# A linear-attention and SwiGLU kernel rewritten in hand order: four tokens per partition, attention pieces in slots beside FFN steps, DMA transposes, two-bank PSUM tiles

## The chip, the cores and the metric

The kernel runs on one core of one Trainium2 chip. The metric is device time in microseconds (us) of one execution; lower is better. Every number below comes from a timed run, from the profile of one execution, or is worked out from such numbers, and the text says how. The profile's span (first to last instruction) is up to 2 us shorter than the time. A run is called slow when it took over 1.5% longer than the fastest run of the same kernel. Verdicts and ratios use the fast runs alone; the medians in the tables are of all runs (the change, e5 and e12 have one slow run of four, e13 has two).

Engines are named as the profile names them: PE is TensorE (matmuls), PEld its weight loads, DVE is VectorE, ACT is ScalarE, POOL is GpSimd, SPq is the queue of SyncE, from which most DMAs are issued. PSUM is the memory that matmuls write into; a tile of 128 x 512 fp32, the size of one accumulator here, is called one bank. To evict a tile is to move its contents from PSUM to the on-chip memory SBUF, which DVE and ACT do here.

## The reference, cut to what matters

Linear attention over 8 batches, 8 heads, 576 tokens, head width 64, and then an RMS norm and a SwiGLU feed-forward network (FFN) over all 4608 tokens, 512 wide inside the model and 1536 wide in the FFN.

```python
def phi(x, c, s):
    r = np.maximum(x, 0.0)
    return np.concatenate([r * c, r * s], axis=-1)      # 64 -> 128 features
q_p, k_p = phi(q, cos_w, sin_w), phi(k, cos_w, sin_w)
kv  = np.einsum('bhsf,bhsd->bhfd', k_p, v)              # "kvz": with sum(k_p) as 65th column
num = np.einsum('bhsf,bhfd->bhsd', q_p, kv)             # "nd": numerator and denominator
x   = num / den, heads side by side                     # 4608 x 512
xn  = x / rms * rms_g
out = (silu(xn @ w_gate) * (xn @ w_val)) @ w_out
```

## The kernel before

The tile framework orders the instructions and sets the waits between engines. The FFN works on blocks of 512 tokens. While block b-1 is in its gate/value steps, batch b's attention and block b-2's output matmuls are interleaved. 576 tokens are 4.5 rows of 128, so batches and blocks don't align.

```python
psmm  = ctx.enter_context(tc.tile_pool(name="psmm", bufs=1, space=PSUM))
psgv  = ctx.enter_context(tc.tile_pool(name="psgv", bufs=2, space=PSUM))   # gps, vps: two tiles each
psacc = ctx.enter_context(tc.tile_pool(name="psacc", bufs=2, space=PSUM))  # acc: two tiles

def attn_kvz(b):                         # [cut] 5 chunks per head; the tail chunk has 64 rows
    for h in range(H):
        for ci, (ti, lane0, clen, s0, col, ridx) in enumerate(chunks):
            nc.tensor.matmul(kvz[:, h, 0 : FA + 1], lhsT=kp[:clen, ci, h, :],
                             rhs=vv[:clen, ci, h, :], start=(ci == 0), stop=(ci == len(chunks) - 1))

def ffn_gval_step(blk, nn, filler_blk=None):            # one of 12 steps of a block
    gps = psgv.tile([P, 512], FP32, name="gps", tag="g")
    vps = psgv.tile([P, 512], FP32, name="vps", tag="v")
    # [cut] 4 matmuls into gps, 4 into vps
    if filler_blk is not None:
        ffn_out_step(filler_blk, 4)                     # 4 output matmuls of an earlier block
    nc.scalar.activation(out=sig[:, :], in_=gps[:, :], func=AF.Sigmoid)
    nc.scalar.copy(out=valc[:, :], in_=vps[:, :])
    nc.vector.tensor_tensor(out=t1[:, :], in0=gps[:, :], in1=sig[:, :], op=ALU.mult)
    nc.gpsimd.tensor_tensor(out=hT[:, nn, :], in0=t1[:, :], in1=valc[:, :], op=ALU.mult)

for b in range(1, B):                                   # [cut]
    attn_prep(b, next_load=b + 1)        # casts, phi; q transposed on TensorE, evicted by DVE
    for nn in range(0, 4):  ffn_gval_step(b - 1, nn, b - 2)
    attn_kvz(b)
    for nn in range(4, 8):  ffn_gval_step(b - 1, nn, b - 2)
    attn_numden(b)
    for nn in range(8, 12): ffn_gval_step(b - 1, nn, b - 2)
    batch_finish()                       # norm; x transposed by DMA
    ffn_out_flush(b - 2)
```

Of the kernel before, what the change touches and what calls it, by code (L numbers as in the profile page):

```python
# [5 lines left out]

# [8 lines left out]
ALU = mybir.AluOpType  # L15


@with_exitstack
def kernel(
# [13 lines left out]
    T = B * S  # L33
# [3 lines left out]
    NTT = T // P  # L37
    TB = 512
    NBLK = T // TB
    NDT = DM // P  # L40
    NNT = DFF // P
    FA = D
    F = 2 * D
    assert B == 8 and H == 8 and S == 576 and D == 64
    inv_dm = 1.0 / DM

    consts = ctx.enter_context(tc.tile_pool(name="consts", bufs=1))
    wts = ctx.enter_context(tc.tile_pool(name="wts", bufs=1))
    raw_pool = ctx.enter_context(tc.tile_pool(name="raw", bufs=1))
    qp_pool = ctx.enter_context(tc.tile_pool(name="qp", bufs=2))  # L50
    kp_pool = ctx.enter_context(tc.tile_pool(name="kp", bufs=1))
    qpt_pool = ctx.enter_context(tc.tile_pool(name="qpt", bufs=1))
    kvz_pool = ctx.enter_context(tc.tile_pool(name="kvzs", bufs=2))
    xt_pool = ctx.enter_context(tc.tile_pool(name="xt", bufs=5))
    small = ctx.enter_context(tc.tile_pool(name="small", bufs=6))
    xn_pool = ctx.enter_context(tc.tile_pool(name="xn", bufs=4))
    xnt_pool = ctx.enter_context(tc.tile_pool(name="xnt", bufs=4))
    scr_pool = ctx.enter_context(tc.tile_pool(name="scrp", bufs=2))
    psmm = ctx.enter_context(tc.tile_pool(name="psmm", bufs=1, space=bass.MemoryType.PSUM))
    psgv = ctx.enter_context(tc.tile_pool(name="psgv", bufs=2, space=bass.MemoryType.PSUM))  # L60
    psacc = ctx.enter_context(tc.tile_pool(name="psacc", bufs=2, space=bass.MemoryType.PSUM))
    late = {}

    even_starts = [0, 128, 256, 384, 512]
    odd_starts = [0, 64, 192, 320, 448]
    s0_list = even_starts + odd_starts
    ncol = len(s0_list)
    iota_i = consts.tile([P, 1], mybir.dt.int32, name="iota_i")
    nc.gpsimd.iota(iota_i[:, :], pattern=[[0, 1]], base=0, channel_multiplier=1)
    iota_f = consts.tile([P, 1], FP32, name="iota_f")  # L70
    nc.vector.tensor_copy(out=iota_f[:, :], in_=iota_i[:, :])
    cos_tab = consts.tile([P, ncol], FP32, name="cos_tab")
    sin_tab = consts.tile([P, ncol], FP32, name="sin_tab")
    th_tab = consts.tile([P, ncol], FP32, name="th_tab")
    cth_tab = consts.tile([P, ncol], FP32, name="cth_tab")
    ang = math.pi / 2.0 / float(S)
    for j, s0 in enumerate(s0_list):
        nc.vector.tensor_scalar(
            out=th_tab[:, j : j + 1], in0=iota_f[:, :], scalar1=float(s0), scalar2=ang,
            op0=ALU.add, op1=ALU.mult,  # L80
        )
    nc.vector.tensor_single_scalar(
        out=th_tab[:, :], in_=th_tab[:, :], scalar=math.pi / 2.0, op=ALU.min
    )
    nc.vector.tensor_single_scalar(
        out=cth_tab[:, :], in_=th_tab[:, :], scalar=math.pi / 2.0, op=ALU.add
    )
    nc.scalar.activation(out=sin_tab[:, :], in_=th_tab[:, :], func=AF.Sin)
    nc.scalar.activation(out=cos_tab[:, :], in_=cth_tab[:, :], func=AF.Sin)
    ident = consts.tile([P, P], BF16, name="ident")  # L90
    masks.make_identity(nc, ident[:, :])

    raw_tiles = {}
    last_load = {}

    def issue_loads(b):
        rq4 = raw_pool.tile([P, 4, H, D], FP32, name="rq4", tag="rq4")
        rk4 = raw_pool.tile([P, 4, H, D], FP32, name="rk4", tag="rk4")
        rv4 = raw_pool.tile([P, 4, H, D], FP32, name="rv4", tag="rv4")
        rq1 = raw_pool.tile([P, H, D], FP32, name="rq1", tag="rq1")  # L100
        rk1 = raw_pool.tile([P, H, D], FP32, name="rk1", tag="rk1")
        rv1 = raw_pool.tile([P, H, D], FP32, name="rv1", tag="rv1")
        if b % 2 == 0:
            s4 = slice(0, 512)
            s1 = slice(512, 576)
        else:
            s1 = slice(0, 64)
            s4 = slice(64, 576)
        for (rr4, rr1, src) in ((rv4, rv1, v), (rk4, rk1, k), (rq4, rq1, q)):
            for c in range(4):  # L110
                s0 = s4.start + c * P
                nc.sync.dma_start(  # L112
                    out=rr4[:, c, :, :],
                    in_=src[b, :, s0 : s0 + P, :].rearrange("h s d -> s h d"),
                )
            ins = nc.sync.dma_start(
                out=rr1[0:64, :, :],
                in_=src[b, :, s1, :].rearrange("h s d -> s h d"),
            )
            last_load[b] = ins  # L120
        raw_tiles[b] = (rq4, rk4, rv4, rq1, rk1, rv1)

    wg = wts.tile([P, NDT, DFF], BF16, name="wg")
    wv = wts.tile([P, NDT, DFF], BF16, name="wv")
    wo = wts.tile([P, NNT, DM], BF16, name="wo")
    rmsg = consts.tile([P, NDT], FP32, name="rmsg")

    def weight_dmas(stage_pool):
        with nc.allow_non_contiguous_dma(reason="small gather of rms_g"):
            nc.sync.dma_start(  # L130
                out=rmsg[:, :], in_=moe_rms_g.rearrange("(t p) -> p t", p=P)
            )
        sgs, svs, sos = [], [], []
        for dt in range(NDT):
            sg = stage_pool.tile([P, DFF], FP32, name=f"sg{dt}", tag=f"sg{dt}")
            nc.sync.dma_start(out=sg[:, :], in_=moe_w_gate[dt * P : (dt + 1) * P, :])
            sgs.append(sg)
        for dt in range(NDT):
            sv = stage_pool.tile([P, DFF], FP32, name=f"sv{dt}", tag=f"sv{dt}")
            nc.sync.dma_start(out=sv[:, :], in_=moe_w_val[dt * P : (dt + 1) * P, :])  # L140
            svs.append(sv)
        for nt3 in range(NNT // 3):
            so = stage_pool.tile([P, 3, DM], FP32, name=f"so{nt3}", tag=f"so{nt3}")
            nc.sync.dma_start(
                out=so[:, :, :],
                in_=moe_w_out[nt3 * 3 * P : (nt3 + 1) * 3 * P, :].rearrange(
                    "(t p) m -> p t m", p=P
                ),
            )
            sos.append(so)  # L150
        return sgs, svs, sos

    def weight_convs(sgs, svs, sos):
        for dt in range(NDT):
            nc.vector.tensor_scalar(
                out=wg[:, dt, :], in0=sgs[dt][:, :], scalar1=rmsg[:, dt : dt + 1],
                scalar2=None, op0=ALU.mult,
            )
        for dt in range(NDT):
            nc.vector.tensor_scalar(  # L160
                out=wv[:, dt, :], in0=svs[dt][:, :], scalar1=rmsg[:, dt : dt + 1],
                scalar2=None, op0=ALU.mult,
            )
        for nt3 in range(NNT // 3):
            nc.scalar.copy(out=wo[:, nt3 * 3 : (nt3 + 1) * 3, :], in_=sos[nt3][:, :, :])

    def chunks_of_batch(b):
        i0 = (9 * b) // 2
        if b % 2 == 0:
            lst = [  # L170
                (i0 + 0, 0, 128, 0, 0, 0),
                (i0 + 1, 0, 128, 128, 1, 1),
                (i0 + 2, 0, 128, 256, 2, 2),
                (i0 + 3, 0, 128, 384, 3, 3),
                (i0 + 4, 0, 64, 512, 4, -1),
            ]
        else:
            lst = [
                (i0 + 0, 64, 64, 0, 5, -1),
                (i0 + 1, 0, 128, 64, 6, 0),  # L180
                (i0 + 2, 0, 128, 192, 7, 1),
                (i0 + 3, 0, 128, 320, 8, 2),
                (i0 + 4, 0, 128, 448, 9, 3),
            ]
        return lst

    xtok = {}
    xt_done = {}
    pending = []
    ssq_cur = {}  # L190
    xnT_blocks = {}
    hT_tiles = {}
    kp_tiles = {}
    vv_tiles = {}
    qpT_tiles = {}
    ssq_tiles = {}
    ksv_tiles = {}

    def ensure_xnT_block(blk):
        if blk not in xnT_blocks:  # L200
            t = xnt_pool.tile([P, NDT, TB], BF16, name=f"xnT_{blk}", tag="xnT")
            xnT_blocks[blk] = t
        return xnT_blocks[blk]

    def tile_complete(i, ssq_b):
        ensure_xnT_block(i // 4)
        col = len(pending)
        pending.append(i)
        xt = xtok[i]
        scr = scr_pool.tile([P, DM], FP32, name="scr", tag="scr")  # L210
# [5 lines left out]
    def batch_finish():  # L216
        tiles = list(pending)
        if not tiles:
            return
# [134 lines left out]
    def ffn_out_step(blk, nsteps):  # L354
# [3 lines left out]
        for _ in range(nsteps):  # L358
            if j >= 4:
                break  # L360
# [123 lines left out]
```

## Time and profile before

| | before |
|---|---|
| time, median of 3 | 423.27 us (422.99 to 423.47) |
| profile's span | 421.9 us |
| first FFN matmul | 65.4 us |
| one batch in steady state | 39.8 us |

The page's first part is the busy time of each engine (us, share of the span, number of instructions):

```profile
PE 345.4 (82%) x2215; PEld 174.3 (41%) x2256; DVE 259.3 (61%) x541; ACT 206.9 (49%) x419; POOL 127.3 (30%) x115
```

82% is an average of two regimes. The windows view gives busy time by stretch (columns: window, its length, then each engine's busy us and instructions, granted TensorE clock, DMA share, GB/s):

```profile
0.00:65.00 65.00, 12.41 (x128) 9.51 (x128) 37.47 (x99) 12.60 (x25) 0.76 (x7) 1.00 1.09 263
...
225.00:265.00 40.00, 38.84 (x269) 19.72 (x273) 30.52 (x63) 22.82 (x49) 15.24 (x13) 1.00 0.57 123
```

For 65 us PE has almost nothing to do, because data and weights are being loaded and prepared. Later it is busy most of the time.

The timeline of PE shows a late stretch in which the FFN runs alone (columns: start us, length us, engine, line, operation, output<-inputs, count, and in brackets the idle time before it and what ended it):

```profile
355.81 1.03 PE L394 MATMUL gps<-xnT_3368,wg 128*128 128x512 bf16 x4
356.68 1.03 PE L402 MATMUL vps<-xnT_3368,wv 128*128 128x512 bf16 x4
357.54 1.03 PE L364 MATMUL acc<-wo,hT 128*128 128x512 bf16 x4
358.40 1.03 PE L394 MATMUL gps<-xnT_3368,wg 128*128 128x512 bf16 x4
```

Read the starts, not the lengths: the length includes the tail of the pipelined matmul. From 355.81 to 356.68 to 357.54 to 358.40 each group of four takes 0.86 us, 216 ns per matmul, and nothing waits. A block of FFN is 144 such matmuls, 31.1 us.

One more line of the timeline, the 40 kvz matmuls of a batch:

```profile
199.18 2.96 PE L303 MATMUL kvz<-vv,kp 128*128 128x65 bf16 x40
```

### The profile page before, as it was taken

What the parts mean: (1) busy time and instruction counts of PE and PEld (TensorE: products, weight loads), DVE (VectorE), ACT (ScalarE), POOL (GpSimd) and SP (SyncE); (2) the same over time, 40 slices, a digit from 0 to 9 for tenths busy, and PEclk for the clock granted to TensorE, in tenths of its full rate; (3) what the DMA queues carried; (4) which work ended last, traced back from release to release, by engine and by line L of the source; (5) the groups of instructions that cost most, each with busy time, mean ns of one, the idle gap of its engine ahead of it and who ended that gap; (6) DMA issues with size and microseconds to landing.
All of it is one profiled execution on the core that took longest, in us unless ns stands there. A gap on an engine that the chain in (4) does not pass through costs nothing.

```text
span 421.9 us, 6418 instructions
## 1 busy us (share of the span) xinstructions
PE 345.4 (82%) x2215; PEld 174.3 (41%) x2256; DVE 259.3 (61%) x541; ACT 206.9 (49%) x419; POOL 127.3 (30%) x115
## 2 busy tenths in 40 slices
PE   0262008969897999979989999899999999999996
PEld 0241005534453445444444544454455444444442
DVE  3857547697469868775888596959681463222210
ACT  1004403546365644754465458544834686555541
POOL 0000001443145333424242434234243434444430
PEclk9999999989999999999999999999999999999999
DMA  9999999970676765736573675450120013010012
GB/s 178 225 416 394 214 176 187 198 155 2 123 170 124 157 152 128 149 86 138 125 164 76 127 163 113 110 115 26 39 63 26 26 50 88 27 50 26 25 50 99
DMA packets 140591, 52.32 MB, mean 124 GB/s; under 512 B 133392, under 2 KB 133392, under 8 KB 140560
## 3 DMA queue, kind: packets, MB, share of 16 engines
q1 hardware_dynamic: 140560, 51.92, 54.7%
q8 instruction: 17, 0.28, 0.3%
q14 instruction: 14, 0.11, 0.1%
HBM read 37.75 MB, written 9.44 MB: 112 GB/s over the span
## 4 chain that ended last, share of the span: by engine, by line
PE 59%; DVE 15%; DMA 11%; ACT 6%; issue 4%; SPq 4%; DVEq 0%; ACTq 0%
PE gps L394 17%; PE acc L364 16%; PE vps L402 15%; PE kvz L303 6%; PE tps L288 4%; SPq L112 3%; DMA rv_271<-in_v_dram 3%; PE nd L323 2%; DVE kp L269 2%; DVE kp L265 2%; DVE qp L278 2%; DVE qpT L291 2%; ACT sig L412 2%; DVE xt L342 1%; DVE xn L233 1%
## 5 line engine op out<-in xcount | busy, mean ns | idle before, releaser
L364 PE MATMUL acc<-wo,hT 128*128 128x512 bf16 x426 | 108.1, 379 | 0.4
L412 ACT ACTIVATE sig<-gps 128x512 bf16<-128x512 f32 x108 | 64.8, 600 | 74.5 <-PE gps L394 67.6
L414 ACT CAST valc<-vps 128x512 bf16<-128x512 f32 x108 | 63.2, 585 | 31.6 <-PE vps L402 30.1
L288 PE MATMUL tps<-ident,qp 128*128 128x128 bf16 (+1 forms) x320 | 26.0, 231 | 45.7 <-DVE qp L282 40.6
L394 PEld LDWEIGHTS <-wg 128*128 128x128 bf16 x432 | 40.4, 99 | 54.6 <-issue 8.9
L402 PEld LDWEIGHTS <-wv 128*128 128x128 bf16 x432 | 41.9, 99 | 47.2 <-issue 1.1
L364 PEld LDWEIGHTS <-hT 128*128 128x128 bf16 x432 | 41.2, 98 | 46.1
L288 PEld LDWEIGHTS <-qp 128*128 128x128 bf16 (+1 forms) x320 | 21.9, 106 | 57.9 <-DVE qp L282 42.6
L211 ACT ACTIVATE scr<-xt 128x512 f32<-128x512 f32 x36 | 22.7, 629 | 18.5 <-DVE xt L342 18.5
L323 PE MATMUL nd<-kvzs,qpT 128*128 128x65 bf16 (+1 forms) x320 | 18.4, 202 | 14.6 <-DVE xt L342 13.5
L374 ACT COPY osb<-acc 128x512 f32<-128x512 f32 x36 | 21.2, 588 | 18.2 <-PE acc L364 18.0
L291 DVE COPY qpT<-tps 128x1024 bf16<-128x1024 bf16 (+1 forms) x40 | 25.3, 633 | 6.7 <-PE tps L288 6.3
L342 DVE TENSOR_TENSOR xt<-nd,rec 128x512 f32<-128x512 f32 (+1 forms) x40 | 27.5, 688 | 1.0
L312 ACT CAST kvzs<-kvz 128x65 bf16<-128x65 f32 x64 | 8.3, 252 | 39.4 <-PE kvz L303 39.4
L323 PEld LDWEIGHTS <-qpT 128*128 128x128 bf16 (+1 forms) x320 | 14.8, 105 | 28.0 <-DVE xt L342 22.7
L303 PE MATMUL kvz<-vv,kp 128*128 128x65 bf16 (+1 forms) x320 | 24.8, 203 | 0.5 <-DVE qpT L291 0.5
L417 POOL TENSOR_TENSOR hT<-t_578,valc 128x512 bf16<-128x512 bf16 x1 | 1.2, 1151 | 70.4 <-DMA rv_547<-in_v_dram 70.4
L303 PEld LDWEIGHTS <-kp 128*128 128x128 bf16 (+1 forms) x320 | 18.1, 99 | 9.5 <-issue 2.6
L412 ACT ACT_TABLE_LOAD x8 | 10.3, 1283 | 22.2 <-PE gps L394 22.1
L233 DVE TENSOR_SCALAR xn<-xt,rs 128x512 bf16<-128x512 f32 x36 | 17.7, 547 | 1.3 <-DMA xnT_3368<-xn 0.6
L337 DVE RECIPROCAL rec<-nd 128x8 f32<-128x8 f32 (+1 forms) x40 | 8.1, 201 | 11.5 <-PE nd L323 11.4
L394 PE MATMUL gps<-xnT_353,wg 128*128 128x512 bf16 x45 | 13.3, 410 | 2.1 <-DMA xnT_353<-xn 1.4
(344 smaller groups left out, 568.6 us busy)
## 6 DMA issues: line engine op xcount, KB each, us to landing
out_dram<-osb SPq DMA_DIRECT2D x36, 256.0 KB, 2.1
rv_133<-in_v_dram SPq DMA_DIRECT2D x4, 256.0 KB, 4.7
rk_132<-in_k_dram SPq DMA_DIRECT2D x4, 256.0 KB, 5.5
rq_131<-in_q_dram SPq DMA_DIRECT2D x4, 256.0 KB, 5.3
rv_271<-in_v_dram SPq DMA_DIRECT2D x4, 256.0 KB, 9.6
rk_270<-in_k_dram SPq DMA_DIRECT2D x4, 256.0 KB, 5.9
rq_269<-in_q_dram SPq DMA_DIRECT2D x4, 256.0 KB, 5.9
rv_544<-in_v_dram SPq DMA_DIRECT2D x4, 256.0 KB, 4.2
```

What stands on the lines that cost most here:

```text
L211: nc.scalar.activation(out=scr[:, :], in_=xt[:, :], func=AF.Square, accum_out=ssq_b[:, col : col + 1])
L233: nc.vector.tensor_scalar(out=xn[:, :], in0=xt[:, :], scalar1=rs[:, jj : jj + 1], scalar2=None, op0=ALU.mult,)
L288: nc.tensor.transpose(tps[:, h, 0:clen], qp[:clen, h, :], ident[:clen, :clen])
L291: nc.vector.tensor_copy(out=qpT[:, :, s0 : s0 + clen], in_=tps[:, :, 0:clen])
L303: nc.tensor.matmul(kvz[:, h, 0 : FA + 1], lhsT=kp[:clen, ci, h, :], rhs=vv[:clen, ci, h, :], start=(ci == 0), stop=(ci == len(chunks) - 1),)
L323: nc.tensor.matmul(nd[lane0 : lane0 + clen, h, 0 : FA + 1], lhsT=qpT[:, h, s0 : s0 + clen], rhs=kvzs[:, h, :], start=True, stop=True,)
L342: nc.vector.tensor_tensor(out=xt3[lane0 : lane0 + clen, :, :], in0=nd[lane0 : lane0 + clen, :, 0:D], in1=rec[lane0 : lane0 + clen, 0:H].un ...
L364: nc.tensor.matmul(acc[:, :], lhsT=hT[:, nn, j * P : (j + 1) * P], rhs=wo[:, nn, :], start=(nn == 0), stop=(nn == NNT - 1),)
L394: nc.tensor.matmul(gps[:, :], lhsT=wg[:, dt, nn * P : (nn + 1) * P], rhs=xnT[:, dt, :], start=(dt == 0), stop=(dt == NDT - 1),)
L402: nc.tensor.matmul(vps[:, :], lhsT=wv[:, dt, nn * P : (nn + 1) * P], rhs=xnT[:, dt, :], start=(dt == 0), stop=(dt == NDT - 1),)
L412: nc.scalar.activation(out=sig[:, :], in_=gps[:, :], func=AF.Sigmoid)
L414: nc.scalar.copy(out=valc[:, :], in_=vps[:, :])
```

## The change

The intent is to rewrite the kernel with the order of instructions set by hand. Each partition holds four consecutive tokens, so loads move runs of 1 KB instead of 256 B. A block is the first 512 tokens of one batch, and the eight remainders of 64 tokens make a ninth, shared block. Attention pieces sit in named slots of the 16 steps of a block (12 gate/value steps, 4 output steps). Sigmoid, copy and two products become one Silu and one product; POOL keeps only the small rsqrt of the norm in the loop. The q transposes of batches 2 to 7 go to the DMA. The weights are cast by the DMA. The tail rows of kvz are padded with zeros to 128. All of PSUM is four tiles of two banks each, used half by half.

The diff, cut to its core:

```diff
+    ctx.enter_context(tc.manual_schedule())
-    psmm = ctx.enter_context(tc.tile_pool(name="psmm", bufs=1, space=bass.MemoryType.PSUM))
-    psgv = ctx.enter_context(tc.tile_pool(name="psgv", bufs=2, space=bass.MemoryType.PSUM))
-    psacc = ctx.enter_context(tc.tile_pool(name="psacc", bufs=2, space=bass.MemoryType.PSUM))
+    ps = ctx.enter_context(tc.tile_pool(name="ps", bufs=1, space=bass.MemoryType.PSUM))
+    psA = ps.tile([P, 2, 512], FP32, name="psA")      # kvz, nd
+    psG = ps.tile([P, 2, 512], FP32, name="psG")      # gate
+    psV = ps.tile([P, 2, 512], FP32, name="psV")      # value
+    psC = ps.tile([P, 2, 512], FP32, name="psC")      # output
@@ [cut: loads] @@
+            in_=src[b, h0:h1, 0:512, :].rearrange("h (p j) d -> p h (j d)", j=4),
@@ [cut: kvz; kpt and vvt are the tail chunk, padded with zeros] @@
+                lhsT = kp_main[b][:, c, h, :] if c < 4 else kpt[b % 2][:, h, :]
+                rhs = vvm[b % 2][:, c, h, :] if c < 4 else vvt[b % 2][:, h, :]
@@ [cut: FFN steps] @@
-        nc.scalar.activation(out=sig[:, :], in_=gps[:, :], func=AF.Sigmoid)
-        nc.scalar.copy(out=valc[:, :], in_=vps[:, :])
-        nc.vector.tensor_tensor(out=t1[:, :], in0=gps[:, :], in1=sig[:, :], op=ALU.mult)
-        nc.gpsimd.tensor_tensor(out=hT[:, nn, :], in0=t1[:, :], in1=valc[:, :], op=ALU.mult)
+        nc.scalar.activation(out=sg[:, :], in_=psG[:, bank, :], func=AF.Silu)
+        nc.vector.tensor_tensor(
+            out=hTs[blk][:, n, :], in0=psV[:, bank, :], in1=sg[:, :], op=ALU.mult)
@@ [cut: slots; k_phi and loads are placed in the same way] @@
+            at(b, qn, "post", q_phi, V, nb, c, 0)
+            at(b, qn, "post", q_phi, A, nb, c, 1)
+            at(b, qn, "post", q_tr_dma, nb, c)
+        at(vb, vn, "post", v_cast, A, nb, LOW)
+        at(vb, vn + 1 if first else vn, "post", v_cast, A, nb, HIGH)
+        at(vb, vn, "post", v_cast_tail, A, nb)
+    def gval_step(blk, n):
+        bank = n % 2
+        run(blk, n, "pe")
+        gval_mm(blk, n, bank)
+        run(blk, n, "pre")
+        sg = gval_act(blk, n, bank)
+        gval_h(blk, n, bank, sg)
+        run(blk, n, "post")
+    def out_step(blk, j):
+        n = 12 + j
+        run(blk, n, "pe")
+        bank = psC[:, j % 2, :]
+        for i in range(NNT):
+            out_mm(blk, j, i, bank)
+        run(blk, n, "pre")
+        out_store(nc.scalar, blk, j, bank)
+        run(blk, n, "post")
+    for blk in range(1, 9):
+        for n in range(NNT):
+            gval_step(blk, n)
+        for j in range(4):
+            out_step(blk, j)
```

## The prediction

> **What bounds it now.** TensorE. The page has PE busy 82% of 421.9 us; the windows show two regimes. Until 65.4 us there is no FFN matmul: PE works about 17 of 70 us. After that PE is busy about 95%, and successive last x transposes (145.9, 184.8, 224.6, 266.0, 303.5, 344.7 us in the timeline) give 39.8 us per batch. In the timeline four 128x512 matmuls take 0.863 us, 216 ns each; the Trainium skill (TensorE: Matmul & The Clock Gate, "Wait — 56ns, not 53.3ns?") states 215.7 ns, and this trace agrees. A block of FFN is 144 of them, 31.1 us; 40 kvz matmuls take 2.9 us; 40 nd 2.2; 40 q transposes 3.0: sum 39.2. So stalls are only about 0.6 us per batch. Nine FFN blocks alone are 280 us.
>
> **What the change does.**
> 1. q transposes leave PE for DMA in batches 2-7: -3.0 us of PE each, 18 us in all. A 128x512 DMA transpose takes 1.22 us of SP's queue; a 128x1024 should take near 2.4. I estimate 17 us of transposes per block plus 5 for loads and stores, of 36: it fits.
> 2. sig, valc, t1, hT become one Silu (ACT, 0.60) and one product (DVE, 0.69). POOL leaves the loop, so the phis that take 1.37 us beside POOL return to 0.48: the Trainium skill (SBUF — State Buffer, Terms, shared port pair) states such blocking; the trace is consistent with it. Table loads (16 x 1.28) go; half of phi moves to ACT. I estimate ACT 190 and DVE 185 us busy: neither binds, so nearly all of this is off the critical path.
> 3. The xnT wait between batches (1-2 us) goes: x is transposed during the output steps. The tail block collects the remainders.
> 4. Opening: 1 KB runs instead of 256 B, weights cast by the DMA, FFN started chunk by chunk. DMA moved 410 GB/s for weights but 180-210 for q, k, v. I estimate batch 0 landed near 13 us, FFN from about 25, then paced by PE and the loads (wo by 50-60 us). Block 0's output with batch 1's attention: 16 us of PE plus 8 of waits (transpose directly behind nd, square, norm). Block 0 done near 77 us; before, at 107, its output projection was still to be done.
>
> **Sum.** 77 (70-85) + 6 blocks x (31.1+2.9+2.2, plus 0.8 of stalls) = 222, + 2 bare blocks 62.2 + last copy and store 3 = 364. Against before: about 40 from the opening, 18 from transposes, the rest waits. Time 364 us, range 350 to 382. Faster by over 2%: 0.96; within 2%: 0.03; slower: 0.01.
>
> **What would show it.** Page: PE busy above 90%, total near 335 us; POOL below 5% after the opening. Timeline: first FFN matmul near 25 us, block 0's last output near 77, period 36-38 us. Chain of waits: almost all PE, DMA only in the first 60 us. Granted clock near 1.
>
> **What would make it wrong.** (a) 128x1024 DMA transposes cost more, or queue behind the 1 MB loads, so nd waits and the period exceeds 38. (b) Casting weight DMAs are slow, or batch 1's loads behind them stop the in-order DVE and ACT in block 0, and it ends past 85. (c) psA is the only buffer for kvz and nd: an nd waits for the eviction before it (0.69 + 0.4). (d) Silu slower, or table reloads. (e) PE idling long enough to lower its clock.

## The result, and the profile after

| | before | after |
|---|---|---|
| time, median | 423.32 us (4 runs) | 412.27 us (409.08 to 415.47, 4 runs; one slow) |
| ratio of fast runs | 1 | 0.972 (95% interval 0.966 to 0.978) |
| profile's span | 421.9 us | 408.5 us |
| mean granted clock in the profile | 0.990 | 0.956 |

Ratios here and below are the mean time of one kernel's fast runs over that of the kernel before in the same rounds, so they are not quite the ratios of the medians quoted. The change is faster, by 2.8% (12 us). The prediction was 364 us, 14% less than before, with 382 as the upper end of its range. Its direction was right; 48 us are missing.

The same line of the page after:

```profile
PE 341.2 (84%) x2085; PEld 162.3 (40%) x2122; DVE 180.1 (44%) x366; ACT 188.5 (46%) x345; POOL 38.3 (9%) x74
```

The predicted engine loads came true (ACT 190, DVE 185, PE about 335), and yet PE is at 84% and not above 90. So the missing time is not work. It is waiting. The windows view for the three stages (up to the end of block 0, blocks 1 to 6 with attention beside them, blocks 7 and 8 alone):

```profile
0.00:91.91 91.91, 62.24 (x485) 35.00 (x492) 43.24 (x97) 37.32 (x71) 22.74 (x46) 0.85 0.81 171
91.91:333.47 241.56, 212.85 (x1322) 99.50 (x1346) 120.29 (x245) 131.54 (x242) 15.59 (x28) 0.99 0.67 148
333.47:408.50 75.03, 66.07 (x282) 27.83 (x286) 16.60 (x24) 19.61 (x33) 0.00 (x0) 0.99 0.11 32
```

Set against the terms of the prediction's sum (starts of the blocks read from the timeline of PE):

| stage | predicted | after |
|---|---|---|
| to the end of block 0 | 77 | 91.9 |
| blocks 1 to 6 | 222 (37.0 each) | 241.4 (40.2 each) |
| blocks 7 and 8 | 62.2 (31.1 each) | 70.4 (35.2 each) |
| last copy and store | 3 | 4.8 |

The third line is the sharpest finding. Blocks 7 and 8 have no attention beside them and no loads to wait for, and still take 35.2 us for 31.1 us of matmuls. The timeline of block 7 answers to the FFN lines shown of before:

```profile
340.66 1.03 PE L372 MATMUL psG<-xnT,wg 128*128 128x512 bf16 x4
...
341.67 1.02 PE L372 MATMUL psV<-xnT,wv 128*128 128x512 bf16 x4
...
342.53 1.03 PE L372 MATMUL psG<-xnT,wg 128*128 128x512 bf16 x4
342.80 0.69 DVE L387 TENSOR_TENSOR hT<-psV,sg 128x512 bf16<-128x512 f32 x1 [1.18 <-PE psV L372]
...
343.55 1.02 PE L372 MATMUL psV<-xnT,wv 128*128 128x512 bf16 x4
```

psG starts at 340.66 and psV at 341.67: 1.01 us, not 0.86. The next psV starts at 343.55, right when the product hT, which reads the previous psV, has ended (342.80 + 0.69 = 343.49). But that product reads the other half of psV. With two halves in turn, psV should wait for the product of two steps ago. A step takes 1.87 us instead of 1.73. The output steps show it more plainly:

```profile
361.87 0.59 ACT L245 COPY osb<-psC 128x512 f32<-128x512 f32 x1 [2.84 <-PE psC L392]
...
362.51 2.75 PE L392 MATMUL psC<-wo,hT 128*128 128x512 bf16 x12 [0.67 <-ACT osb L245]
...
365.93 2.75 PE L392 MATMUL psC<-wo,hT 128*128 128x512 bf16 x12 [0.67 <-ACT osb L245]
```

Each output step takes 3.42 us (362.51 to 365.93) for twelve matmuls that need 2.59 us. PE waits until the copy of the previous accumulator has ended, although the next accumulator is the other half of psC.

A third wait stands at the start of every block from 2 to 7:

```profile
210.18 1.03 PE L372 MATMUL psG<-xnT,wg 128*128 128x512 bf16 x4
...
210.99 2.00 ACT L245 CAST vvm<-rv 128x1024 bf16<-128x1024 f32 x2
...
213.01 0.62 ACT L245 CAST vvt<-rvt 64x512 bf16<-64x512 f32 x1
213.65 0.60 ACT L381 ACTIVATE sg<-psG 128x512 f32<-128x512 f32 x1
...
214.30 1.05 PE L372 MATMUL psG<-xnT,wg 128*128 128x512 bf16 x4 [2.23 <-ACT sg L381]
```

The gate of step 0 is ready at about 211.2, but ACT works in order, and the v casts of a later batch stand ahead of the Silu. The next psG waits for that Silu, again one of the other half.

The waits view of PE ranks them (waiter <- what ended the wait: us in total, times, longest):

```profile
PE psC L392 <- ACT osb L245: 15.0, 24, 0.7
PE psG L372 <- ACT sg L381: 12.4, 7, 2.2
PE psV L358 <- DVE xn L333: 9.7, 4, 2.7
...
PE psV L372 <- DVE hT L387: 2.7, 7, 0.5
```

The view understates the last of these: a wait shorter than the modelled tail of the matmul before it is not counted as idle, and so the 0.15 us per gate/value step appear only in the starts.

The waits in the compiled program, which can be rebuilt from the kernel without a chip, say the same. Matmuls are named by tile and bank:

```
changed kernel   matmul psG bank 1 (step 1)  waits for  Silu of step 0, which reads psG bank 0
                 matmul psV bank 1 (step 1)  waits for  product of step 0, which reads psV bank 0
                 matmul psC bank 1           waits for  copy of psC bank 0
```

In the kernel before, a matmul into gps waits for the product that read that same buffer two steps earlier.

So the theory to test: the framework guards a PSUM tile as one thing, and a tile of two banks used half by half is a single buffer. Two rivals: the loss comes from ACT's in-order queue alone, or from the lower granted clock.

### The profile page after: what moved, and what is told of

It reads as the page before. It is cut to its first block, busy times and chain, and to the rows that moved or that the text cites. A ratio compares the mean times of both kernels' runs of the same rounds, so it can differ in the third digit from the quotient of the medians.

```text
span 408.5 us, 5622 instructions
## 1 busy us (share of the span) xinstructions
PE 341.2 (84%) x2085; PEld 162.3 (40%) x2122; DVE 180.1 (44%) x366; ACT 188.5 (46%) x345; POOL 38.3 (9%) x74
## 4 chain that ended last, share of the span: by engine, by line
PE 67%; DVE 10%; ACT 10%; issue 5%; DMA 5%; POOL 2%; SPq 1%; DVEq 0%; ACTq 0%
PE psC L392 22%; PE psV L372 20%; PE psG L372 18%; ACT osb L245 4%; DVE xn L333 3%; DVE xt L309 2%; PE psA L269 2%; DMA wv<-in_moe_w_val_dram 2%; DMA rv<-in_v_dram 2%; DVE hT L387 2%; ACT vvm L245 2%; PE psA L284 2%; PE psG L392 1%; ACT sg L381 1%; DMA qpT<-qp 1%
## 5 line engine op out<-in xcount | busy, mean ns | idle before, releaser
L387 DVE TENSOR_TENSOR hT<-psV,sg 128x512 bf16<-128x512 f32 x108 | 74.5, 691 | 157.8 <-PE psV L372 98.2
L372 PE MATMUL psG<-xnT,wg 128*128 128x512 bf16 (+1 forms) x392 | 100.4, 375 | 14.5 <-ACT sg L381 12.4
L392 PE MATMUL psC<-wo,hT 128*128 128x512 bf16 x398 | 95.3, 381 | 15.7 <-ACT osb L245 15.0
L381 ACT ACTIVATE sg<-psG 128x512 f32<-128x512 f32 x108 | 64.3, 596 | 85.7 <-PE psG L372 84.3
L372 PE MATMUL psV<-xnT,wv 128*128 128x512 bf16 (+1 forms) x400 | 100.8, 374 | 2.9 <-DVE hT L387 2.7
L245 ACT COPY osb<-psC 128x512 f32<-128x512 f32 x33 | 19.3, 586 | 66.6 <-PE psC L392 66.6
L333 DVE SCALAR_TENSOR_TENSOR xn<-xt,rs,gb 128x512 bf16<-128x512 f32 x36 | 26.9, 746 | 22.9 <-POOL rs L326 22.9
L321 ACT ACTIVATE scr<-xt 128x513 bf16<-128x513 f32 x36 | 22.9, 637 | 24.6 <-DVE xt L309 24.4
L309 DVE TENSOR_TENSOR xt<-psA,rec 128x512 f32<-128x512 f32 x34 | 23.5, 691 | 1.2
L185 ACT ACTIVATE qp<-rq,tab 128x512 bf16<-128x512 f32 (+1 forms) x34 | 22.5, 676 | 1.2 <-DMA rq<-in_q_dram 1.1
L185 ACT ACTIVATE kpm<-rk,tab 128x512 bf16<-128x512 f32 (+1 forms) x34 | 21.1, 675 | 1.8 <-DMA rk<-in_k_dram 1.8
```

The lines of the kernel that those rows point to most:

```text
L185: nc.scalar.activation(out=out_ap, in_=in_ap, func=AF.Relu, scale=scale)
L245: nc.scalar.copy(out=o, in_=i)
L309: nc.vector.tensor_tensor(out=xt[:, 0:DM].rearrange("p (b h d) -> p b h d", b=2, d=D), in0=o[:, :, :, 0:D], in1=rec[:, :, :].unsqueeze(3). ...
L321: nc.scalar.activation(out=scr[:, :], in_=xt[:, 0 : DM + 1], func=AF.Square, scale=1.0 / math.sqrt(DM), accum_out=ms[:, :],)
L333: nc.vector.scalar_tensor_tensor(out=xn[:, :], in0=x_of[(b, j)][:, 0:DM], scalar=rs_of[(b, j)][:, :], in1=gb[:, :], op0=ALU.mult, op1=ALU. ...
L372: nc.tensor.matmul(pst[:, bank, cols[0] : cols[1]], lhsT=w[:, t, n * P : (n + 1) * P], rhs=x[:, t, cols[0] : cols[1]], start=(t == 0), sto ...
```

## The experiments

Fourteen kernels ran; all gave correct results. e1 to e4 shared one chip, e5 to e8 the next job, e9 to e12 a third, e13 and e14 a fourth; each has four runs, beside seven of the kernel before.

| run | what it is | median us | ratio to before |
|---|---|---|---|
| | the change | 412.27 | 0.972 |
| e1 | psG, psV, psC split into one-bank tiles | 370.48 | 0.876 |
| e2 | psC alone split | 392.58 | 0.930 |
| e3 | psG and psV alone split | 388.01 | 0.917 |
| e4 | v casts on DVE, tiles as in the change | 397.24 | 0.941 |
| e5 | e1 + v casts on DVE | 366.53 | 0.868 |
| e6 | e1 + two changes in the opening | 359.56 | 0.850 |
| e7 | e1, kvz tail on 64 rows | 384.82 | 0.910 |
| e8 | e1, q transposes on TensorE | 443.57 | 1.052 |
| e9 | e8 with phi earlier | 399.54 | 0.946 |
| e10 | e1 + e4 + e6 | 358.18 | 0.848 |
| e11 | the kernel before, kvz tail padded to 128 rows | 419.72 | 0.993 |
| e12 | e10 + psA split | 358.42 | 0.845 |
| e13 | e9 with v casts on DVE | 383.48 | 0.898 |
| e14 | the kernel before, with two-bank tiles | 442.56 | 1.048 |

### e1: one tile per bank

```diff
+class Banks:
+    def __init__(self, tiles): self.tiles = tiles
+    def __getitem__(self, key): return self.tiles[key[1]][(key[0],) + tuple(key[2:])]
-    psG = ps.tile([P, 2, 512], FP32, name="psG")
+    psG = Banks([ps.tile([P, 512], FP32, name=f"psG{i}") for i in range(2)])
     # the same for psV and psC
```

The same banks, the same order, the same arithmetic; only the names under which the framework keeps them differ. (In the opening two evictions read both banks of psC; each becomes five DVE instructions instead of three.)

> psG, psV and psC become two one-bank tiles each; order and arithmetic as in the changed kernel. Theory BANKS (a two-bank PSUM tile is tracked as one, so a matmul into one half waits for the reader of the other half): out steps fall from 3.42 to 2.6 us (34 of them, -28), gate/value steps from 1.87 to 1.73 (-15), the wait behind ACT's v casts is partly absorbed: 412 -> about 370 (362 to 380), period of a full block from 40.3 to about 35. Rival ACT ORDER (the loss is ACT's in-order queue: v casts and evictions ahead of Silu): stays above 400. Rival CLOCK (the loss is the lower granted clock alone): stays above 400 and the clock stays near 0.95.

Measured: 370.48 us, ratio 0.876 (0.872 to 0.879). BANKS holds and both rivals fall: ACT's order is unchanged, and the clock in the profile is 0.947, no higher than the change's 0.956. In its compiled program a matmul into the second psG tile waits for the Silu of two steps before, which read that tile. In its timeline of PE the FFN is as dense as in the kernel before:

```profile
319.76 1.03 PE L398 MATMUL psV<-xnT,wv 128*128 128x512 bf16 x4
320.62 1.03 PE L398 MATMUL psG<-xnT,wg 128*128 128x512 bf16 x4
321.48 1.03 PE L398 MATMUL psV<-xnT,wv 128*128 128x512 bf16 x4
322.35 3.83 PE L418 MATMUL psC<-wo,hT 128*128 128x512 bf16 x17
```

Starts are 0.86 us apart, and output steps follow each other without a gap. Block 7 takes 31.1 us (35.2 in the change), blocks 1 to 6 take 34.75 us on average (40.2). The opening is no better: block 0 ends at 93.1 us.

### e2 and e3: each half of the split alone

The edit is that of e1, for psC alone (e2) and for psG and psV alone (e3).

> Only psC (output accumulators) is split. BANKS: -28 us, about 384 (378 to 392); osb waits of PE gone (15.0 us), gate/value steps still 1.87. ACT ORDER and CLOCK: about 412, since ACT's work and order are the same.

> Only psG and psV are split. BANKS: gate/value steps 1.73 instead of 1.87 (-15), and the 2.2 us wait for the first Silu of a block is hidden mostly (-8 to -13): about 388 (380 to 398); out steps still 3.42. ACT ORDER and CLOCK: above 400.

Measured: e2 392.58 us (ratio 0.930), e3 388.01 us (0.917). e2 gained less than I had written, and ends 0.6 us outside its range. The expectation charged every one of 34 output steps with 0.83 us, but the first output step of a block doesn't wait, and the waits view counts 24 such waits. Block 7 goes from 35.2 to 32.7 us: 2.5 us per block, not 3.3. The two savings add up: against the change's 0.972, e2 saves 0.042 and e3 0.055 of the time of before, together 0.097, and e1 saves 0.096.

### e4 and e5: the v casts

```diff
-        at(vb, vn, "post", v_cast, A, nb, LOW)
-        at(vb, vn + 1 if first else vn, "post", v_cast, A, nb, HIGH)
-        at(vb, vn, "post", v_cast_tail, A, nb)
+        at(vb, vn, "post", v_cast, V, nb, LOW)
+        at(vb, vn + 1 if first else vn, "post", v_cast, V, nb, HIGH)
+        at(vb, vn, "post", v_cast_tail, V, nb)
```

> Tiles as in the changed kernel; the v casts of batches 2 to 7 go from ACT to DVE, which is idle at the end of a block. BANKS: saves the 2.2 us wait at the start of six blocks and the half-clock stretch that follows some of them: 412 -> about 396 (390 to 402), steps otherwise as before (3.42 and 1.87). ACT ORDER: nearly the whole loss goes, below 385. CLOCK: clock up to 0.97 and about 400.

> The split of e1 and the v casts on DVE of e4 together. BANKS: with true double buffering the late first Silu of a block is already hidden (the wait of psG for sg is 2.7 us in all in e1's profile), so only -2 to -5 against e1: about 367 (363 to 371). If the two savings were independent (44 and 15), it would be about 355.

Measured: e4 397.24 us (ratio 0.941), as BANKS had it: every block from 1 to 6 takes 37.9 us, where the change takes 38.4 to 41.7, and block 7 stays at 35.2. (CLOCK had named about 400 and a clock of 0.97 for e4; 0.963 came. So e4 by itself doesn't tell CLOCK from BANKS; e1 does, where the time fell by 41 us and the clock did not rise.) e5 gives 366.53 us (0.868), 4 us below e1. So, by the ratios, the casts ahead of the Silu cost 13 us beside the two-bank tiles, and only 4 once the tiles are split: with true double buffering PE has a step of slack, in which a late Silu does little harm. The wait was real in the change, but the tiles had made it dear.

### e6: the opening

The last four weight DMAs are issued on POOL behind batch 0's first two rsqrt. In block 0's output phase nd runs one step earlier, and the transpose that needs its result stands four steps behind it (three for the last) instead of one.

```diff
-    for i in range(1, 6):
+    for i in range(1, 4):
         gval_slice(256 * i, 256 * i + 256)
@@
     x_sq(0, 0)
+    gval_slice(1024, 1280)
@@
     x_sq(0, 1)
+    gval_slice(1280, 1536)
@@ block 0's output phase
-        if n in (4, 6, 8, 10):                 # nd, eviction, square, norm
+        if n in (3, 5, 7, 9):
-        if n in (5, 7, 9, 11):                 # transpose of xn, eviction
+        if n in (7, 9, 11):                    # the fourth behind the loop
```

> e1 with two changes up to block 0's end: the last four weight DMAs are issued on POOL behind batch 0's first two rsqrt (now they wait 3.4 us behind DMAs[...]), and in block 0's output phase nd runs one step earlier and its transpose two steps later, so that the chain eviction, square, pow, norm (3.9 us) is covered by matmuls. If these waits (6.8 and 8.8 us of PE in e1's profile) and the half clock after them make the opening long, block 0 ends 8 to 13 us earlier: about 360 (356 to 364). Rival LOADS (the opening waits for HBM data anyway): no change, 370.

Measured: 359.56 us, 11 us below e1. In its timeline block 0's last output matmuls start at 78.7 us and block 1 at 82.9, where e1's block 1 starts at 93.1. So for these 11 us waits in my own order of the opening, and not the loads, were the cause; LOADS falls for them. No run separates the two parts. The one profile of each gives a reading: the output phase of block 0 starts at 63.2 us in e6 and 66.6 in e1, and takes 19.7 and 26.5 us, so the larger part (6.8 of 10.2 us) comes with the output phase. The half rate of PE early in the opening is in both.

### e7: the height of the kvz tail

```diff
-                lhsT = kp_main[b][:, c, h, :] if c < 4 else kpt[b % 2][:, h, :]
-                rhs = vvm[b % 2][:, c, h, :] if c < 4 else vvt[b % 2][:, h, :]
+                lhsT = kp_main[b][:, c, h, :] if c < 4 else kpt[b % 2][lo:hi, h, :]
+                rhs = vvm[b % 2][:, c, h, :] if c < 4 else vvt[b % 2][lo:hi, h, :]
```

> e1 with the tail matmuls of kvz on their 64 real rows instead of 128 rows with zeros, as the kernel before has it. If mixing 64-row and 128-row weights is what makes 40 kvz matmuls 2.9 us before and 1.2 us after: kvz goes back to about 2.9 us and the time rises by 8 x 1.65 = 13 us to about 383 (378 to 388). If the faster kvz comes from layout or order: no change, 370.

Measured: 384.82 us, 14 us above e1. The timeline of one head in the change, with 128 rows throughout:

```profile
183.38 0.29 PE L269 MATMUL psA<-vvm,kpm 128*128 128x65 bf16 x4
183.50 0.19 PE L269 MATMUL psA<-vvt,kpt 128*128 128x65 bf16 x1
183.53 0.29 PE L269 MATMUL psA<-vvm,kpm 128*128 128x65 bf16 x4
```

The next lines are the same view of e7, PE alone. There the fifth matmul of the head has 64 rows:

```profile
182.07 0.29 PE L281 MATMUL psA<-vvm,kpm 128*128 128x65 bf16 x4
182.29 0.20 PE L281 MATMUL psA<-vvt,kpt 64*128 64x65 bf16 x1
182.42 0.30 PE L281 MATMUL psA<-vvm,kpm 128*128 128x65 bf16 x4
```

Read from start to start of the groups of four, a head takes 0.15 us in the change (183.38 to 183.53) and 0.35 us in e7 (182.07 to 182.42). All 40 matmuls take 1.21 us in the change (the gate matmuls follow at 184.59) and 2.88 us in e7 (they follow at 184.95). The Trainium skill (TensorEngine Tiling (Array Packing), Key Properties) states "Mode switching requires drain". The traces are consistent with it, and put a number on a change of height: the group of 64 rows starts 0.22 us after the group of four before it (0.12 with 128 rows), and the next group 0.13 us after that (0.03). Over the batch, (2.88 - 1.21) / 16 switches is 0.10 us each. That the time is spent on a drain is not shown. The blocks with attention agree: from block 2 on they take 1.7 us more each than in e1.

### e8, e9 and e13: q transposes back on TensorE

```diff
 e8:
-            at(b, qn, "post", q_tr_dma, nb, c)
+            at(b, qn + 1, "pe", q_tr_pe, nb, c, psA[:, c % 2, :])
+            at(b, qn + 1, "pre", q_tr_evac, V, nb, c, psA[:, c % 2, :])
 e9, on top: q_phi at the head of the step
-            at(b, qn, "post", q_phi, V, nb, c, 0)
-            at(b, qn, "post", q_phi, A, nb, c, 1)
+            at(b, qn, "pe", q_phi, V, nb, c, 0)
+            at(b, qn, "pe", q_phi, A, nb, c, 1)
 e13, on top: the v casts on DVE, as in e4
```

In all three, block 1's q pieces also start one step earlier.

> e1 with the q transposes of batches 2 to 7 back on TensorE (five per batch into psA, evicted by DVE) instead of DMA. By the prediction's term 3.0 us of PE per batch come back, +18: 388; by the 0.44 us per eight that the traces show, 2.0 to 2.2 per batch, +12 to +13: about 383 (378 to 388). Rival (the DMA transposes delay nd and loads as much as they save): no change or faster.

> e8 cost 73 us, of which transposes themselves are about 13; its trace shows PE waiting 1.3 us for qp before each transpose, because the phi stands behind the step's last product in DVE's and ACT's order. Here the phi is issued at the head of the step, so it is done when the next step's transpose needs it. If e8's excess is that placement: about 383 (377 to 392) against e1's 370, the transposes' own cost. If DMA transposes are worth more than that (PSUM traffic, psA shared with kvz and nd): stays above 410.

> e9's TensorE transposes with the v casts on DVE, against e5 (366.5), which has the DMA transposes and the same v casts. e9's trace still has 11 us of waits of the first transpose of a block for qp, whose phi stands behind the v casts on ACT. If that was e9's remaining excess: transposes alone, +12 to +14, about 380 (375 to 387). If TensorE transposes cost more than their own 2.2 us per batch in this layout whatever the order: stays above 393.

Measured: 443.57, 399.54 and 383.48 us. e8 missed every expectation by 55 us. Its timeline shows why: the transpose stands at the head of a step, and the phi that it needs was queued behind the previous step's product, which itself ends only after that step's matmuls.

```profile
200.34 0.48 DVE L196 TENSOR_SCALAR qp<-rq,tab 128x512 bf16<-128x512 f32 x1
...
200.96 0.61 PE L245 MATMUL psA<-ident,qp 128*128 128x128 bf16 x8 [1.34 <-DVE qp L196]
```

PE stands still 1.34 us in each such step, and part of the steps run at half rate after it. e9 moves the phi and recovers 44 us, but misses its range (377 to 392) by 8 us and stays below the 410 of its rival; it still has 11 us of waits for the first phi of a block, behind ACT's v casts. e13 takes those away and lands inside its range. Its profile and one other run are slow. The fast runs' ratio, 0.898, stands 0.031 above e5's 0.868, or 13 us of before's 423. That is what the DMA transposes are worth, 2.2 us per batch (two fast runs stand behind it; in the profiles four of the six blocks with attention differ by 2.2 us each). The price is paid in DMA time, and it is not small: in blocks 1 to 6 the windows view has a DMA share of 0.80 in e5 and 0.49 in e13, which is 57 us more of busy DMA engines (0.80 x 206.9 less 0.49 x 221.7). PE does not wait for it: the waits view of PE in e5 names no DMA. The queue time is small. The page's last part lists the issues (count, then the median time from issue to landing):

```profile
qpT<-qp SPq DMA_TRANSPOSE x30, 3.9
xnT<-xn SPq DMA_TRANSPOSE x24, 2.4
```

A 128x1024 transpose (six of the 30 have 64 rows) lands 3.9 us after its issue, and, by the view of that tile, holds SP's queue for 1.26 us at the median (1.20 to 4.90), hardly longer than the 1.22 us of a 128x512. I had expected 2.4.

### e10 and e12: the combination

e10 joins the edits of e1, e4 and e6. e12 also splits psA by the edit of e1.

> Split banks, v casts on DVE and the changed opening together: e6's 359.6 less the 3 to 4 us that e5 showed against e1: about 356 (353 to 360), faster than both kernels of the case.

> e10 with psA split as well: kvz, nd and the transposes use single banks, the eviction becomes five DVE instructions instead of three. BANKS: removes false waits around kvz and in the opening, 2 to 5 us: about 353 (350 to 357). If psA's waits are true dependencies (nd waits for the eviction of the same data): 356, no change, or 1 us more for DVE's extra instructions.

Measured: 358.18 and 358.42 us, ratios 0.848 (0.845 to 0.851) and 0.845 (0.840 to 0.850). They are not told apart from each other, nor from e6 (0.850) with certainty. e12 misses the 350 to 357 of BANKS: splitting psA brought nothing measurable. The waits of nd for the eviction of psA stay (5.3 us in e10, 4.5 in e12), so they are mainly true dependencies, as the second theory had it. Each of the two beats both kernels: about 15% faster than before and 13% faster than the change.

### e11: padding in the kernel before

```diff
+        for ci, (ti, lane0, clen, s0, col, ridx) in enumerate(chunks):     # in attn_prep
+            if clen < P:
+                nc.gpsimd.memset(kp[clen:P, ci, :, :], 0.0)
+                nc.gpsimd.memset(vv[clen:P, ci, :, :], 0.0)
-                    lhsT=kp[:clen, ci, h, :],
-                    rhs=vv[:clen, ci, h, :],
+                    lhsT=kp[:, ci, h, :],
+                    rhs=vv[:, ci, h, :],
```

> The kernel before with one thing changed: the 64-row tail chunk of kvz is filled up to 128 rows with zeros (memsets on POOL at the head of each batch) and multiplied at full height. If 64-row weights between 128-row ones cost what e7 showed: kvz from 2.9 to 1.2 us, 8 x 1.65 = 13 us, 423 -> about 410 (407 to 415). If the memsets on POOL or other waits take it back: 418 to 425.

Measured: 419.72 us, ratio 0.993. The mechanism acted: in its chain of waits kvz takes 1.22 us per batch, which saves 13 us of PE in all. But only 3 us arrive. The chain then has more of DVE and DMA in it (DVE 21% and DMA 13%, where before has 15% and 11%), with phis such as this one, which take 0.48 us at other times:

```profile
206.46 1.29 DVE kp L273
```

So the kernel before is not bound by TensorE as firmly as I had taken it to be: PE time taken away came back as waits for others. It is not that the memsets slow the phis: the phis take 100 us of DVE in both kernels, and the long ones run beside POOL's product hT in both (the one shown beside the hT from 206.21 to 207.48). What grew is the v casts, which run beside the memsets: 40 of them take about 17 us before (0.42 each) and 24.8 in e11, nearly all of DVE's rise from 259.3 to 268.7 us. How much of the lost gain this explains, no run tests alone.

### e14: the fault alone, in the kernel before

```diff
-    psgv = ctx.enter_context(tc.tile_pool(name="psgv", bufs=2, space=bass.MemoryType.PSUM))
-    psacc = ctx.enter_context(tc.tile_pool(name="psacc", bufs=2, space=bass.MemoryType.PSUM))
+    psgv = ctx.enter_context(tc.tile_pool(name="psgv", bufs=1, space=bass.MemoryType.PSUM))
+    gps2 = psgv.tile([P, 2, 512], FP32, name="gps2")      # likewise vps2, acc2
-        gps = psgv.tile([P, 512], FP32, name="gps", tag="g")
+        gps = gps2[:, nn % 2, :]                          # likewise vps, acc
```

> The fault of the change alone, put into the kernel before: its double-buffered gps, vps and acc become halves of two-bank tiles used in turn. BANKS: matmuls into one half wait for the reader of the other; where output matmuls stand between gate/value steps part is hidden, so +8 to +35 us: about 440 (431 to 458). If two-bank tiles cost nothing by themselves and the fault needs the hand order: 423, no change.

Measured: 442.56 us, ratio 1.048 (1.041 to 1.054), 20 us slower than before. The two-bank tile alone makes a loss, without the hand order. Two things differ in this run, though: the framework also places the instructions anew when the waits change. The waits view of PE has the new waits, which were below 1 us in all before:

```profile
PE gps L396 <- DVE t L418: 11.3, 18, 1.1
...
PE acc L366 <- ACT osb L376: 6.3, 7, 1.5
```

## Why the prediction was wrong

The change is faster, as predicted with 0.96, but by 12 us and not by 59. The step that failed is the sum, "6 blocks x (31.1+2.9+2.2, plus 0.8 of stalls) = 222, + 2 bare blocks 62.2": it took PE to run the FFN without gaps, 0.8 us of stalls per block. In its place the runs show false waits of 41 us. I read `bank = n % 2` in the diff as double buffering, as the two tiles of the pool before had been. The list of what could go wrong names psA as a single buffer, and not psG, psV and psC.

The e1 run sets the parts apart (all from the timelines of PE):

| stage | predicted | the change | e1, tiles split |
|---|---|---|---|
| to the end of block 0 | 77 | 91.9 | 93.1 |
| blocks 1 to 6 | 222 | 241.4 | 208.5 |
| blocks 7 and 8 | 62.2 | 70.4 | 62.2 |
| last copy and store | 3 | 4.8 | 4.7 |
| sum (span) | 364 | 408.5 | 368.5 |

- **False waits between the halves of a two-bank tile: 41 us** (0.972 - 0.876 of 423), not in the prediction at all. Shown by e1, taken apart by e2 and e3, and put into the kernel before by e14. Part of it is the late Silu behind the v casts (13 us beside two-bank tiles by e4, 4 without by e5).
- **The opening: 15 us longer than predicted.** The estimate of 8 us for the chain of nd, square, norm and transpose in block 0's output was about right (four waits, 9.7 us); what I had not costed was batch 0's rsqrt, queued on POOL behind the weight DMAs, and PE at half rate between about 15 and 34 us. In the change the output phase starts at 64.1 us, where the prediction's terms put it at 53 (77 less 16 and 8), and takes 27.8 us instead of 24. e6 gains 11 us in the opening; what the half rate alone costs there is not separated.
- **Attention on PE: cheaper than predicted by 2.6 us per block.** I took 2.9 us for kvz and 2.2 for nd from durations and rates of before. The padded kvz takes 1.2 us (e7 shows why), and eight nd matmuls take 0.26 us from start to start, so 40 take 1.3. In e1 this makes up for most of the opening, and the near match of 368.5 with 364 is two errors that cancel.
- **q transposes: right in kind, too large in size.** Predicted 18 us (3.0 per batch); e13 against e5 shows 13 (2.2 per batch). The SP queue has room for them, as predicted. Worry (a), that nd waits for them, did not show: the waits view of PE has no nd waiting for a DMA. (The chain of waits names a q transpose once, 3.9 us in block 5, but an nd started at 271.62 us, before it landed.)
- **"What bounds it now: TensorE", with 0.6 us of stalls per batch: too simple.** With the measured 1.3 us for nd and 2.2 for the transposes the sum of PE work is about 37.5 of 39.8 us, and e11 got back only 3 of 13 us that were taken from PE.
- **Silu, one product, the elementwise work off POOL: as predicted.** Silu takes 0.60 us, the product 0.69, and the DVE phis stay at 0.48 us in the loop. One table load is left, at the start. POOL keeps the rsqrt: 15.6 us in blocks 1 to 6.
- **The clock (worry (e)): small after the opening.** It is 0.99 in blocks 1 to 6 and 0.85 up to the end of block 0. In the change, blocks 4 and 6 take 41.7 us where blocks 3 and 5 take 39.8; in both the matmuls after the 2.23 us wait run at half rate for some us. Block 2 has the same wait without it and takes 40.2, so this costs about 1.5 us a time.

What stays open: which of e6's two parts gives how much beyond the reading of one profile each, what the half rate costs in the opening, what binds the kernel before once kvz is cheap, and how much of the opening that remains in e10 (about 80 us) could go.

## What to carry to other kernels

Before believing in a double buffer, look at the waits of the compiled program or at the starts of successive matmuls: a buffer's halves are two buffers only if the framework keeps them as two. If all engines are at the predicted load and the kernel is late, look for waits that no data needs, first in a stretch where nothing else runs; a short experiment that renames tiles and changes nothing else settles it. And check small matmuls for changes of row height between neighbours: zeros up to the full height can be cheaper than skipping them (1.2 us against 2.9 here), but the gain arrives only where PE is what the kernel waits for.

## What the Trainium skill lacked or had wrong

- PSUM — Partial Sum Buffer (Summary: rules for kernel authors) advises to target a different bank when PSUM is read while a matmul runs, and to guard by bank. The banks here were different, and 41 us were lost because the guard was set by tile. That a tile of several banks may be guarded as one is on no page that I read.
- TensorEngine Tiling (Array Packing), Key Properties, says that a change of mode drains the TensorE, without a cost: e7 shows 0.10 us per switch between 128 and 64 rows, 1.67 us for the 16 of a batch.
- TensorE: Matmul & The Clock Gate (Part 1) ties the half rate to idle windows of about 3.4 us. In the change, a wait of 2.23 us was followed by matmuls at half rate in two blocks (4 and 6) and, with the same wait, not in block 2. The page calls the window free-running, which may be why; no run here tests it.
- DMA: Bandwidth & Descriptors gives a bandwidth for DMA transposes, not the time from issue to landing of one: here 1.22 us in the queue and 2.4 to landing for 128x512 in bf16, 1.26 and 3.9 for 128x1024 (medians).
